# Long convolution with gate: how the last six results of the first phase reach the first two loads of the middle phase

## The chip, the cores and the metric

The kernel runs on one core of one Trainium2 chip. Five engines work side by side, each through its own list in order: TensorE (PE, with its weight loads PEld), VectorE (DVE), ScalarE (ACT), GpSimd (POOL) and SyncE (SP). SP, ACT and POOL issue DMAs, each on a queue of its own (in the profile q1 is SP's, q10 ACT's, q0 POOL's); all three queues are served by the same 16 DMA engines. The metric is the device time of one execution in microseconds (us).

## The reference, cut to what matters

```
h_filt = relu(pos_emb @ w1) @ w2 * exp(-0.01 * pos)      # a filter as long as the sequence
u      = x * v                                           # batch 4, sequence 12800, 128 channels
y      = irfft(rfft(u, 2S) * rfft(h_filt, 2S))[:S]       # long convolution, by FFT
x1     = x * y
gate   = sigmoid(causal conv of x1, 5 taps);  out = (gate * (x1 @ w_val)) @ w_out
```

The kernel computes the FFTs as matrix products in two steps: the sequence is cut into 2 halves (J) x 100 (N1) x 64 (N2).

## The kernel before

The program has three phases, each with an order written out by hand.

**First phase** (`signal()` and `filt()`, interleaved step by step). `signal()` runs over n = 0..63 (called n2). For each n, `prep(n)` makes the products and their sums and differences on DVE, PE transforms over N1 (L392, `fp`), ACT copies the two PSUM tiles into a result tile `st` of 128 partitions x 2 x 1024 (L393), and the tile goes to the DRAM tensor `a_u`. `a_u` is indexed [k, row, 1024] with k = 0..99; n fills the two rows `n%2*64 + n//2*2` and the next, so even n fill rows 0 to 63 and odd n rows 64 to 127. The 100 values of k stand scattered over the 128 partitions of `st` (PARTS: 64 of them in every second partition, 32 in every fourth, 4 in every 32nd), so a store is three DMAs: 64 k's by ACT and 32 by POOL (L401), and 4 by POOL an n later (L416, `flush`). For the last two n the store of ACT is cut: k = 0..3 go by SP, the other 60 by ACT. Two result tiles are not of the rotating `st` buffers: n = 61 writes into a spare input buffer (`xv_104` below) and n = 63 into the load buffer `ld_78`.

**Middle phase.** It runs over p = 0..49, pairs of k (2p and 2p+1). `load_a(p, parts)` (L198) loads k = 2p, 2p+1 of `a_u` into one of six buffers `ld`, 4 KB for each row and k; `spectrum` multiplies on PE (L492, `z_ps`): its first half uses partitions 0 to 63 (the even n), its second half partitions 64 to 127 (the odd n). DVE multiplies the result with the filter's spectrum (`times`, L498: `va`, `vb`, `vc`, `vd`), POOL adds (L579, L582), PE transforms back (L508, L531), POOL combines (L543), and the results go to the DRAM tensors `c_y` and `c_z`. One p takes DVE about 6.7 us.

**The border.** Pairs 0 and 1 are loaded in four DMAs each: EARLY is rows 0 to 55 and 64 to 119 (all n up to 55), LATE the rest. Pair 0's EARLY loads stand in SP's list at n = 58. LATE of pair 0 and all of pair 1 stand behind the first phase (p = -1), then pairs 2 and 3 whole. Also at p = -1, PE has the filter of pair 0 (`filter_pair`, L473) and ten products that only keep it busy (L565, `w_ps`) in front of `spectrum(0, 0)`. SP runs its list in order: a DMA that waits holds all behind it.

**Last phase**: it reads `c_y` and `c_z`, transforms over N1, and does gate, value and output products. The change doesn't touch it.

Of the kernel before, what the change touches and what calls it, by code (L numbers as in the profile page):

```python
# [24 lines left out]
J, N1, N2 = 2, 100, 64  # L25
# [6 lines left out]
PARTS = ((0, 64, 2, 0), (64, 32, 4, 1), (96, 4, 32, 3))  # L32
# [86 lines left out]
def tile_longconv_gate(  # L119
# [20 lines left out]
    nc = tc.nc  # L140
# [27 lines left out]
    def buffer(until):  # L168
        i = min(free_at, key=free_at.get)
        free_at[i] = until  # L170
        return LD[i]
# [14 lines left out]
    BD = B * D  # L186
    NP = N1 // 2
    PG = KG // 2
    EARLY, LATE = (slice(0, 56), slice(64, 120)), (slice(56, 64), slice(120, 128))
    weights, loaded = {}, {}  # L190

    def load_w(p):
        n_p = min(PG, NP - p)
        wt = buffer(p + n_p + 0.9)[:, 0:PG * 3 * 128].rearrange("p (k c e) -> p k c e", k=PG, c=3)
        nc.sync.dma_start(out=wt[:, 0:n_p], in_=t_w[:, p:p + n_p])
        weights[p // PG] = wt

    def load_a(p, parts, eng=nc.sync):  # L198
        if p not in loaded:
            loaded[p] = buffer(p - 0.2).rearrange("p (k j e) -> p k j e", k=2, j=J)  # L200
        a2 = loaded[p]
        eng.dma_start(
            out=a2[parts].rearrange("p k j e -> p k (j e)"),
            in_=a_u[2 * p:2 * p + 2, parts].rearrange("k p e -> p k e"))
# [5 lines left out]
    with tc.tile_pool(name="p1", bufs=1) as p1, tc.tile_pool(name="ps1", bufs=1, space=PSUM) as ps1:  # L210
# [10 lines left out]
        def load_pos(c0):  # L221
            if c0 < N2:
                for j in range(J):
                    sync_s.dma_start(out=pos_at(c0)[:, j], in_=pos_v[j][:, c0:c0 + HC])
# [83 lines left out]
        def fetch(upto=N2):  # L308
            while ring and fetched[0] < upto:
                i, t = ring.pop(0)  # L310
                n = fetched[0]
                for k0, k, step, p0 in PARTS:
                    nc.sync.dma_start(out=t[p0:p0 + step * (k - 1) + 1:step], in_=xv[n, k0:k0 + k])
                ahead.append((i, t))
                if i < 4:
                    free_at[i] = n - 2 * N2
                fetched[0] += 1
# [40 lines left out]
        def signal():  # L358
            fetch(4)
            load_pos(0)  # L360
            fetch()
            load_pos(HC)
            ready = [prep(0)]
            for n in range(N2):
                if n == 8:
                    nc.gpsimd.dma_start(out=dft, in_=t_dft)
                    nc.gpsimd.dma_start(out=tw, in_=t_tw)
                    nc.gpsimd.dma_start(out=inv, in_=t_inv)
                if n == 12:
                    for dst, src in ((wval, w_val), (wout, w_out), (cw, conv_w.rearrange("k d -> d k"))):  # L370
                        raw = p1.tile(list(dst.shape), mybir.dt.int64, name=f"raw{len(raws)}")
                        nc.gpsimd.dma_start(out=raw, in_=src)
                        raws.append((dst, raw))
                if n in (18, 22, 26):
                    _narrow(nc, p1, *raws[n // 4 - 4])
                if n == BACK + 2:
                    load_w(0)
                if n == N2 - 6:
                    for part in EARLY:
                        load_a(0, part)  # L380
                if n + 1 < N2:
                    ready.append(prep(n + 1))
                both = ready.pop(0)
                if n in SPARE:
                    st = next(t for i, t in ring if i == SPARE[n]).rearrange("p (c e) -> p c e", c=2)
                else:
                    st = p1.tile([128, 2, J * BD], F32, name="st", bufs=4)
                for c in range(2):
                    fp = ps1.tile([128, J, BD], F32, name="fp", bufs=2)
                    for j in range(J):  # L390
                        h = slice(j * 64, j * 64 + 64)
                        nc.tensor.matmul(out=fp[:, j], lhsT=fsd[h, c], rhs=both[c][h], start=True, stop=True)  # L392
                    nc.scalar.copy(out=st[:, c], in_=fp.rearrange("k j e -> k (j e)"))  # L393
                    yield
                src = st.rearrange("k c e -> k (c e)")
                row = n % 2 * N2 + n // 2 * 2
                dst = a_u[:, row:row + 2].rearrange("k c e -> k (c e)")
                for eng, (k0, k, step, p0) in zip((nc.scalar, nc.gpsimd), PARTS):
                    cuts = [0, 4, k] if k0 == 0 and n >= N2 - 2 else [0, k]
                    for a, b in zip(cuts, cuts[1:]):  # L400
                        (nc.sync if b == 4 else eng).dma_start(  # L401
                            out=dst[k0 + a:k0 + b], in_=src[p0 + step * a:p0 + step * (b - 1) + 1:step])
                if n % 2 == 1:
                    release()
                rest.append((dst, src))
                if len(rest) > 1 or n + 1 == N2:
                    flush()

        rest, raws = [], []
        SPARE = {N2 - 3: 6, N2 - 1: 3}  # L410

        def flush():
# [50 lines left out]
    with tc.tile_pool(name="p2", bufs=1, reuse_waits="tile") as p2, \  # L463
# [20 lines left out]
        def new_z():  # L484
            return ps2.tile([128, 2, BD], F32, name="z_ps", bufs=2)
# [67 lines left out]
        with tc.manual_schedule():  # L553
            for p in range(-1, NP + 2):
                now, nxt, old = 0 <= p < NP, p + 1 < NP, 0 <= p - 1 < NP
                if p < 0:
                    z_first = new_z()
                    for part in LATE:
                        load_a(0, part)
                    for part in EARLY + LATE:  # L560
                        load_a(1, part)
                    filt_p[0] = filter_pair(0)
                    for _ in range(10):
                        w_ps = ps2.tile([128, 2, BD], F32, name="c_ps", bufs=2)
                        nc.tensor.matmul(  # L565
                            out=w_ps[:, 0, 0:2 * D], lhsT=ident, rhs=dft.rearrange("p a k -> p (a k)"), start=True, stop=True)
                if (p + 3) % PG == 0 and p + 3 < NP:
                    load_w(p + 3)
                for q in range(2, AHEAD) if p < 0 else (p + AHEAD,):
                    if q < NP:  # L570
                        load_a(q, slice(0, 2 * N2))
                if now:
                    h = filt_p.pop(p)
                    z0, z1 = z_p.pop((p, 0)), z_p.pop((p, 1))
                    va = p2.tile([128, 2 * J, B, D], F32, name="va", bufs=3)
                    vb = p2.tile([128, 2 * J, B, D], F32, name="vb", bufs=2)
                    times(va, z0[:, 0], h[:, 0], 2 * J)
                    times(vb, z0[:, 1], h[:, 1], 2 * J)
                    (nc.gpsimd if nxt else nc.vector).tensor_tensor(va[:, 0:2], va[:, 0:2], vb[:, 0:2], op=ALU.add)  # L579
                    apart = p % 6 == 5  # L580
                    if not apart:
                        nc.gpsimd.tensor_tensor(va[:, 2:4], va[:, 2:4], vb[:, 2:4], op=ALU.add)  # L582
                if nxt:
                    z_p[p + 1, 0] = spectrum(p + 1, 0, z_first if p < 0 else None)
                if now:
                    vc = p2.tile([128, 2, B, D], F32, name="vc", bufs=2)
                    vd = p2.tile([128, 2, B, D], F32, name="vd", bufs=2)
                    times(vc, z1[:, 0], h[:, 0, 0:2], 2)
                    times(vd, z1[:, 1], h[:, 1, 0:2], 2)
                    v_p[p] = [va[:, 2:4]] + [vb[:, 2:4]] * apart + [vc, vd]  # L590
                if now and not nxt:
                    inverse(p, va[:, 0:2])
                if old:
                    inverse_half(p - 1, v_p.pop(p - 1))
                if p + 2 < NP:
                    filt_p[p + 2] = filter_pair(p + 2)
                if nxt:
                    z_p[p + 1, 1] = spectrum(p + 1, 1)
                if now and nxt:
                    inverse(p, va[:, 0:2])  # L600
                if 0 <= p - 2:
                    butterfly(p - 2)
                for s, c, i in early.get(p, ()):
                    load_part(s, c, i)
# [9 lines left out]
    with tc.tile_pool(name="p3", bufs=1, reuse_waits="tile") as p3, \  # L614
# [154 lines left out]
        with tc.manual_schedule():  # L769
# [10 lines left out]
            for i in range(-LEAD, (NT - 1) * R):  # L780
                t, r = divmod(i, R)
                s, q = divmod(i + LEAD, R)
                if q == 0 and s < NT:
                    if 3 <= s + 1 < NT:
                        load_rows(s + 1, (0, 1, 2))
                    j, g = y_order[s]
# [22 lines left out]
                if t + 1 >= 0:  # L809
                    j, g = groups[t + 1]  # L810
# [9 lines left out]
            t = NT - 1  # L820
# [63 lines left out]
```

## Time and profile before

| what | us |
|---|---|
| device time, median of 3 runs (1063.89 to 1065.49) | 1064.03 |
| the profiled execution's own device time | 1066.52 |
| its span, first to last instruction | 1064.7 |
| PE busy, share of the span | 978.8 (92%) |
| DVE busy | 966.9 (91%) |
| POOL busy | 747.9 (70%) |
| ACT busy | 649.2 (61%) |
| first product of the middle phase on DVE starts at | 323.58 |
| last product of the middle phase on DVE starts at | 671.96 |

All times below are us from the start of the span, of this one execution. A row of the timeline gives start, duration, engine, line, operation, what is written and read, and how often; in brackets the idle time of the engine before it and what ended it. An engine name with a q (SPq, ACTq) is that engine's sequencer, which issues DMAs. A row of the chain of waits gives start, duration and what the time was spent on. A row of the table by stretches gives, behind the stretch, its length, then the busy time of PE, PEld, DVE, ACT and POOL, then the granted clock of TensorE, the mean busy share of the 16 DMA engines, and GB/s.

### The profile page before, as it was taken

What the parts mean: (1) busy time and instruction counts of PE and PEld (TensorE: products, weight loads), DVE (VectorE), ACT (ScalarE), POOL (GpSimd) and SP (SyncE); (2) the same over time, 40 slices, a digit from 0 to 9 for tenths busy, and PEclk for the clock granted to TensorE, in tenths of its full rate; (3) what the DMA queues carried; (4) which work ended last, traced back from release to release, by engine and by line L of the source; (5) the groups of instructions that cost most, each with busy time, mean ns of one, the idle gap of its engine ahead of it and who ended that gap; (6) DMA issues with size and microseconds to landing.
All of it is one profiled execution on the core that took longest, in us unless ns stands there. A gap on an engine that the chain in (4) does not pass through costs nothing.

```text
span 1064.7 us, 21554 instructions
## 1 busy us (share of the span) xinstructions
PE 978.8 (92%) x8100; PEld 515.6 (48%) x8100; DVE 966.9 (91%) x933; ACT 649.2 (61%) x1145; POOL 747.9 (70%) x465
## 2 busy tenths in 40 slices
PE   2778799999988999999999999689999999999996
PEld 0344466566644545555445545334444444444442
DVE  8878999699948999999989999369999999999997
ACT  1445577788852444444444434277887888878784
POOL 2232222222225999999899999679999999999990
PEclk9989899999997999999999999899999999999999
DMA  8999899988989889989999997977888888888813
GB/s 286 383 352 375 330 381 373 397 315 327 393 273 306 318 302 334 341 314 339 333 311 342 345 334 259 333 285 270 312 286 300 284 295 306 282 299 296 299 72 124
DMA packets 97152, 330.16 MB, mean 310 GB/s; under 512 B 12691, under 2 KB 37883, under 8 KB 81051
## 3 DMA queue, kind: packets, MB, share of 16 engines
q1 hardware_dynamic: 41864, 196.96, 54.1%
q10 hardware_dynamic: 49506, 111.30, 27.0%
q0 software_dynamic: 5680, 20.53, 5.1%
q8 instruction: 66, 1.08, 0.4%
q14 instruction: 36, 0.29, 0.1%
HBM read 197.67 MB, written 131.07 MB: 309 GB/s over the span
## 4 chain that ended last, share of the span: by engine, by line
PE 65%; DMA 13%; DVE 7%; POOL 5%; ACT 4%; issue 4%; SPq 1%; ACTq 1%; DVEq 0%; POOLq 0%
PE sd L672 11%; PE o_ps L738 8%; PE v_ps L728 7%; PE c_ps L531 7%; PE fp L392 6%; PE tp L684 6%; PE c_ps L508 6%; PE z_ps L492 5%; DMA xv<-in_xv_dram 4%; DMA ld<-in_xv_dram 3%; PE gp L293 3%; PE ap L267 3%; DMA c_z<-c_both 2%; DVE vb L498 2%; POOL c_both L543 2%
## 5 line engine op out<-in xcount | busy, mean ns | idle before, releaser
L699 POOL TENSOR_TENSOR ext<-yr,xr 128x400 f32<-128x400 f32 x120 | 308.3, 2570 | 23.2 <-DVE yr L697 10.8
L716 DVE SCALAR_TENSOR_TENSOR gt<-ext,cw,gt 128x1600 f32<-128x1600 f32 (+1 forms) x132 | 242.3, 1835 | 0.1
L401 POOL DMA_DIRECT2D a_u<-st x62 | 33.3, 537 | 222.9 <-ACT st L393 219.1
L393 ACT COPY st<-fp 128x1024 f32<-128x1024 f32 x124 | 125.7, 1029 | 81.6 <-PE fp L392 41.4
L672 PE MATMUL sd<-ld,inv 128*64 128x512 f32 x512 | 128.0, 619 | 7.2 <-DMA ld<-c_y 6.7
L543 POOL TENSOR_TENSOR c_both<-c_raw 128x512 f32<-128x512 f32 x100 | 126.6, 1295 | 9.9 <-DMA c_z<-c_both 6.4
L536 ACT COPY c_raw<-c_ps 128x1024 f32<-128x1024 f32 x50 | 50.8, 1015 | 135.3 <-PE c_ps L531 117.9
L498 DVE TENSOR_TENSOR va<-z_ps,h_sb 128x2048 f32<-128x2048 f32 x50 | 114.1, 2282 | 19.7 <-PE z_ps L492 19.6
L579 POOL TENSOR_TENSOR va<-va,vb 128x1024 f32<-128x1024 f32 x49 | 117.0, 2387 | 20.4 <-DVE vb L498 20.4
L498 DVE TENSOR_TENSOR vb<-z_ps,h_sb 128x2048 f32<-128x2048 f32 x50 | 114.2, 2284 | 12.8 <-POOL va L582 12.8
L492 PE MATMUL z_ps<-ld,ld 64*64 64x512 f32 x800 | 111.6, 614 | 10.2 <-DVE vb L498 6.1
L392 PE MATMUL fp<-ld,fsd 64*128 64x512 f32 x320 | 89.4, 663 | 27.3 <-DVE ld L343 14.5
L738 PE MATMUL o_ps<-gd,wout 128*128 128x400 f32 x256 | 107.8, 503 | 6.1 <-DVE gd L733 4.6
L677 ACT COPY sd_sb<-sd 128x512 f32<-128x512 f32 x128 | 76.9, 601 | 49.4 <-PE sd L672 37.8
L728 PE MATMUL v_ps<-ext,wval 128*128 128x400 f32 x252 | 105.4, 501 | 0.0
L508 PE MATMUL c_ps<-va,ld 64*64 64x512 f32 x800 | 98.1, 604 | 4.0 <-POOL va L579 2.5
L582 POOL TENSOR_TENSOR va<-va,vb 128x1024 f32<-128x1024 f32 x42 | 101.0, 2406 | 0.0
L684 PEld LDWEIGHTS tp<-ident,sd_sb 128*128 128x128 f32 x512 | 58.3, 140 | 77.8 <-PE sd L672 45.4
L697 DVE TENSOR_TENSOR yr<-tp,dif 128x400 f32<-128x400 f32 x128 | 72.5, 566 | 25.8 <-ACT dif L687 21.6
L514 ACT COPY c_sb<-c_ps 128x1024 f32<-128x1024 f32 x49 | 49.7, 1014 | 59.5 <-PE c_ps L508 59.5
L684 PE MATMUL tp<-ident,sd_sb 128*128 128x128 f32 x512 | 80.0, 280 | 4.0 <-DVE yr L697 4.0
L733 DVE TENSOR_TENSOR gd<-v_ps,sg 128x400 f32<-128x400 f32 x126 | 71.4, 567 | 0.2 <-ACT sg L721 0.2
(116 smaller groups left out, 1817.7 us busy)
## 6 DMA issues: line engine op xcount, KB each, us to landing
ld<-a_u SPq DMA_DIRECT2D x48, 1024.0 KB
a_u<-st ACTq DMA_DIRECT2D x61, 512.0 KB
xr<-in_xt_dram SPq DMA_DIRECT2D x32, 800.0 KB
c_y<-c_sb ACTq DMA_DIRECT2D x49, 512.0 KB
out_dram<-o_sb ACTq DMA_DIRECT2D x31, 800.0 KB
c_z<-c_both ACTq DMA_DIRECT2D x48, 512.0 KB
ld<-in_xv_dram SPq DMA_DIRECT2D x40, 512.0 KB
ld<-c_y SPq DMA_DIRECT2D x32, 512.0 KB
```

What stands on the lines that cost most here:

```text
L392: nc.tensor.matmul(out=fp[:, j], lhsT=fsd[h, c], rhs=both[c][h], start=True, stop=True)
L393: nc.scalar.copy(out=st[:, c], in_=fp.rearrange("k j e -> k (j e)"))
L492: nc.tensor.matmul(out=z[half[h], c], lhsT=wk[half[c], 0, half[h]], rhs=a2[half[c], h, j], start=True, stop=True)
L498: nc.vector.tensor_tensor(out, z.rearrange("p (b d) -> p b d", d=D).unsqueeze(1).to_broadcast([128, n, B, D]), h_sb.unsqueeze(2).to_broadc ...
L508: nc.tensor.matmul(out=c_ps[half[m], h], lhsT=wk[half[h], 1 + c, half[m]], rhs=vt[half[h], c].rearrange("p b d -> p (b d)"), start=(c == 0 ...
L543: nc.gpsimd.tensor_tensor(both[:, :, m], raw[:, :, 1], raw[:, :, 0], op=op)
L672: nc.tensor.matmul(out=to, lhsT=inv[:, 2 if j * m * c else c], rhs=t, start=True, stop=True)
L684: nc.tensor.transpose(out=tp[:, b], in_=t[:, b], identity=ident)
L699: nc.gpsimd.tensor_tensor(e[:, r0 + r], yr, xr, op=ALU.mult)
L716: nc.vector.scalar_tensor_tensor(gt, rows(t, k)[:, cols], cw[:, k:k + 1], gt, op0=ALU.mult, op1=ALU.add)
L728: nc.tensor.matmul(out=v_ps, lhsT=wval, rhs=rows(t)[:, r * ROW:(r + 1) * ROW], start=True, stop=True)
L738: nc.tensor.matmul(out=o_ps, lhsT=wout, rhs=gd, start=True, stop=True)
```

## The change

EARLY becomes rows 0 to 57 and 64 to 121 (all n up to 57), and LATE is gone. For n = 58 to 63, the four k's of pairs 0 and 1 no longer go through `a_u`: SP copies them from the result tile straight into the two load buffers, four DMAs for each n (k = 0..3), each of one partition of the tile into two partitions (2 x 4 KB). Pair 0's EARLY loads stand in SP's list at n = 60 (before: n = 58), then the copies of n = 58, 59 and 60, then pair 1's EARLY loads (before: behind the first phase), then the copies of n = 61, 62 and 63. The stores of n = 58 to 63 to `a_u` leave out k = 0..3; from n = 60 on ACT issues none of them and POOL all; those of n = 62 stand behind the tile of n = 63.

```diff
-    EARLY, LATE = (slice(0, 56), slice(64, 120)), (slice(56, 64), slice(120, 128))
+    EARLY = slice(0, 58), slice(64, 122)
...
+    def new_a(p):
+        loaded[p] = buffer(p - 0.2).rearrange("p (k j e) -> p k j e", k=2, j=J)
...
-                if n == N2 - 6:
+                if n in (N2 - 4, N2 - 3):
                     for part in EARLY:
-                        load_a(0, part)
+                        load_a(n - N2 + 4, part)
...
-                for eng, (k0, k, step, p0) in zip((nc.scalar, nc.gpsimd), PARTS):
-                    cuts = [0, 4, k] if k0 == 0 and n >= N2 - 2 else [0, k]
-                    for a, b in zip(cuts, cuts[1:]):
-                        (nc.sync if b == 4 else eng).dma_start(
-                            out=dst[k0 + a:k0 + b], in_=src[p0 + step * a:p0 + step * (b - 1) + 1:step])
+                if n >= N2 - 6:
+                    direct.append((row, st))
+                while direct and n >= N2 - 4:
+                    at, t = direct.pop(0)
+                    for k in range(4):
+                        if k // 2 not in loaded:
+                            new_a(k // 2)
+                        nc.sync.dma_start(
+                            out=loaded[k // 2][at:at + 2, k % 2].rearrange("c j e -> c (j e)"), in_=t[2 * k:2 * k + 1])
+                held.append((dst, src))
+                while held and not n == N2 - 2:
+                    d, u = held.pop(0)
+                    for eng, (k0, k, step, p0) in zip((nc.scalar if n < N2 - 4 else nc.gpsimd, nc.gpsimd), PARTS):
+                        a = 4 if k0 == 0 and n >= N2 - 6 else 0
+                        eng.dma_start(out=d[k0 + a:k0 + k], in_=u[p0 + step * a:p0 + step * (k - 1) + 1:step])
...
-                    for part in LATE:
-                        load_a(0, part)
-                    for part in EARLY + LATE:
-                        load_a(1, part)
```

SP's list at the border before, from pair 0's EARLY loads on. `ld_80` is pair 0's buffer, `ld_77` pair 1's, `ld_78` first the tile of n = 63 and then pair 2's buffer. DMAHW0 to DMAHW7 are the eight counters on which the DMAs of SP and ACT report their landing, taken in turn; a DMA waits until the one that used its counter before has landed:

```order
L202 DMA ld_80<-a_u 56x2x1024 [waits DMAHW6_49,DMAHW3_49]
L202 DMA ld_80<-a_u 56x2x1024 [waits DMAHW4_49,DMAHW2_49]
L401 DMA a_u<-st 4x2048 [waits DMAHW2_49,Activation_49]
L202 DMA ld_80<-a_u 8x2x1024 [waits DMAHW6_49,DMAHW5_49,DMAHW7_49,DMAHW3_49,DMAHW2_49]
L401 DMA a_u<-ld_78 4x2048 [waits DVE_49,Activation_49]
L202 DMA ld_80<-a_u 8x2x1024 [waits DMAHW6_49,DMAHW5_49,DMAHW0_49]
L202 DMA ld_77<-a_u 56x2x1024 x2
L202 DMA ld_77<-a_u 8x2x1024 [waits DMAHW1_49]
```

The same place of SP's list now (L205 is `load_a`, L408 the new copies): pair 0's two loads and the copies of n = 58 and 59:

```order
L205 DMA ld_80<-a_u 58x2x1024 [waits DMAHW6_49,DMAHW3_49]
L205 DMA ld_80<-a_u 58x2x1024 [waits DMAHW4_49,DMAHW2_49]
L408 DMA ld_80<-st 2x1x1024 [waits Activation_49]
L408 DMA ld_80<-st 2x1x1024 [waits DMAHW7_49]
L408 DMA ld_77<-st 2x1x1024 [waits DMAHW0_49]
L408 DMA ld_77<-st 2x1x1024 [waits DMAHW1_49]
L408 DMA ld_80<-st 2x1x1024 [waits DMAHW3_49,Activation_49]
L408 DMA ld_80<-st 2x1x1024 [waits DMAHW4_49]
```

The last two rows take the counters DMAHW3 and DMAHW4 of the two loads at the top, and so wait for these to land. The copies of n = 60 follow; then come pair 1's loads and the copies of n = 61 (`xv_104`), 62 (`st`) and, of n = 63 (`ld_78`), those for pair 0:

```order
L205 DMA ld_77<-a_u 58x2x1024 [waits DMAHW3_49]
L205 DMA ld_77<-a_u 58x2x1024 [waits DMAHW4_49]
L408 DMA ld_80<-xv_104 2x1x1024 [waits DMAHW5_49,DVE_49,Activation_49]
L408 DMA ld_80<-xv_104 2x1x1024 [waits DMAHW6_49]
L408 DMA ld_77<-xv_104 2x1x1024 [waits DMAHW7_49]
L408 DMA ld_77<-xv_104 2x1x1024 [waits DMAHW0_49]
L408 DMA ld_80<-st 2x1x1024 [waits DMAHW1_49,Activation_49]
L408 DMA ld_80<-st 2x1x1024 [waits DMAHW2_49]
L408 DMA ld_77<-st 2x1x1024 [waits DMAHW3_49]
L408 DMA ld_77<-st 2x1x1024 [waits DMAHW4_49]
L408 DMA ld_80<-ld_78 2x1x1024 [waits DMAHW5_49,DVE_49,Activation_49]
L408 DMA ld_80<-ld_78 2x1x1024 [waits DMAHW6_49]
```

Here too the copies of n = 62 for pair 1 wait on DMAHW3 and DMAHW4, which are pair 1's two loads now, and the copies of n = 63 for pair 0 stand behind them. Eight DMAs of rows that lay behind the first phase have become 4 loads and 24 copies inside it; on PE and DVE the order of instructions is the same as before.

More of the change, by code (lines that the diff above doesn't have):

```diff
@@ L196, in load_w @@
         weights[p // PG] = wt
+    def new_a(p):
+        loaded[p] = buffer(p - 0.2).rearrange("p (k j e) -> p k j e", k=2, j=J)
     def load_a(p, parts, eng=nc.sync):
         if p not in loaded:
-            loaded[p] = buffer(p - 0.2).rearrange("p (k j e) -> p k j e", k=2, j=J)
+            new_a(p)
         a2 = loaded[p]
@@ L407, in signal @@
                     flush()
-        rest, raws = [], []
+        rest, raws, held, direct = [], [], [], []
         SPARE = {N2 - 3: 6, N2 - 1: 3}
```

## The prediction

> **What bounds the kernel now.** I read the chain of waits first, at the border of first and middle phase, since the change moves nothing else. Columns: start, duration, what.
>
> ```profile
> 310.50 1.03 ACT ld L393
> 311.53 0.02 issue
> 311.55 5.47 DMA a_u<-ld
> 317.01 0.02 SPq L202
> ...
> 317.06 4.30 DMA ld<-a_u
> 321.36 0.14 issue
> 321.50 0.48 PE z_ps L492
> ```
>
> The last result tile (n = 63) is ready at 311.53. Then SP's store of its k = 0..3 takes 5.47 us to land, pair 0's last load of 8 rows takes 4.30 us, and only then PE does the second half of the first spectrum, at 321.50. The timeline of DVE and PE says who waits:
>
> ```profile
> 313.67 2.86 PE L565 MATMUL c_ps<-dft,ident 128*128 128x256 f32 x12 [0.52 <-ACT h_sb L481]
> 316.46 1.07 PE L492 MATMUL z_ps<-ld,ld 64*64 64x512 f32 x4
> 323.58 2.29 DVE L498 TENSOR_TENSOR va<-z_ps,h_sb 128x2048 f32<-128x2048 f32 x1 [18.87 <-PE z_ps L492]
> ```
>
> DVE stands still for 18.87 us until 323.58. What it starts then is the bound of the next 350 us, as the groups of DVE over the middle phase show:
>
> ```profile
> L498 DVE TENSOR_TENSOR vb<-z_ps,h_sb 128x2048 f32<-128x2048 f32 x50 | 114.2, 2284 | 12.8 <-POOL va L582 12.8
> L498 DVE TENSOR_TENSOR va<-z_ps,h_sb 128x2048 f32<-128x2048 f32 x50 | 114.1, 2282 | 19.7 <-PE z_ps L492 19.6
> ```
>
> Of the 19.7 us of `va`, 18.87 are the border; beyond it DVE idles some 13.7 us in 350, and waits for POOL then, which hangs on DVE in turn. So **a shift of 323.58 shifts the end by as much**, and the question is only when pair 0's last rows (those of n = 63) are in its buffer.
>
> **What the change removes.** The round trip through DRAM, 5.47 + 4.30 us, is replaced by one copy inside the core. If that were all, the limit would be PE's busy-keeping products, which end at 316.46 here and some 2 us earlier where ACT issues no stores, and the end would come up to 9 us sooner. But the copies of n = 63 stand last in SP's list, and four loads have come in front of them.
>
> **What the loads cost.** How a DMA spreads over the 16 engines can be counted: each engine that takes part adds one small packet to mark its end. Of the first 4 us of the program and of a stretch of the middle phase, the DMA view gives (queue: packets, MB, share of 16 engines):
>
> ```profile
> q10 hardware_dynamic: 364, 0.30, 23.4%
> ...
> fsd<-in_tab_sd_dram ACTq DMA_DIRECT2D x1, 128.0 KB
> fwd<-in_tab_fwd_dram ACTq DMA_DIRECT2D x1, 117.2 KB
> win<-in_tab_win_dram ACTq DMA_DIRECT2D x1, 50.0 KB
> ```
>
> ```profile
> DMA packets 720, 3.01 MB, mean 402 GB/s; under 512 B 48, under 2 KB 48, under 8 KB 720
> ...
> q1 hardware_dynamic: 720, 3.01, 101.5%
> ```
>
> In the second, three loads of 128 rows make 48 marks, 16 each. In the first, `fsd` has 128 rows and `fwd` and `win` 100 each, 328 packets of data; the other 36 are marks: 16 + 10 + 10. So 100 rows went over 10 engines, not 16: rows are dealt in equal whole shares. 56 rows then go over 14 engines (14 x 4), and the table by stretches, while pair 1's two loads of 56 rows were alone in front (DMA share and GB/s are last), agrees:
>
> ```profile
> 320.00:321.00 1.00, 0.00 (x0) 0.00 (x0) 0.00 (x0) 0.00 (x0) 0.00 (x0) 0.67 0.87 197
> 322.00:323.00 1.00, 1.00 (x10) 0.49 (x6) 0.00 (x0) 0.00 (x0) 0.00 (x0) 0.50 0.88 188
> ```
>
> 14/16 is 0.875; and since both loads were queued, the second didn't use the two engines that the first left idle: DMAs of one width take the same engines. **58 is 2 x 29; the only equal shares up to 16 are 2.** So each of the four new loads would run on two engines, the same two, and so would the 24 copies of two rows, queued behind them.
>
> The Trainium skill, page "DMA: Bandwidth & Descriptors", section "Why a DMA increments its semaphore by 16 and not by 1", says the same in general: a DMA uses the largest number of engines up to 16 that divides its slowest dimension, on SP's and ACT's queues the lowest-numbered ones. By that rule 58 rows get 2 engines, always the same; this trace agrees with it for 128, 100 and 56 rows, and shows no DMA of 58.
>
> The price: a load of 58 rows x 2 x 4 KB is 475 KB, 238 KB on each of two engines. The stretch above moved 402 GB/s at a share of 101.5%, so 24.8 GB/s by engine: **9.6 us a load**, 38.4 for four. A fast end is 26.5 GB/s, from the first phase:
>
> ```profile
> 265.00:270.00 5.00, 5.00 (x35) 3.42 (x32) 4.97 (x8) 4.57 (x9) 1.11 (x2) 1.00 1.01 424
> ```
>
> That makes 9.0 us a load, 2.5 less in all. The slow end takes 14 engines at 197 GB/s, 14.1 each, as above: 16.9 us a load, 29 more in all. I take 9.6, of whole loads of the same 4 KB rows; in the slow row 14 engines write one half of the partitions at once, two would not press as hard.
>
> **The sum.** The two new loads of pair 0 need the stores of n = 56 and 57. When that of n = 57 lands is told by SP's own wait for that counter in the present kernel; the other rows are SP's issues, and landings of stores:
>
> ```profile
> 291.44 2.17 SPq L202 DMA_DIRECT2D ld<-a_u  x2
> L401 SPq EVENT_SEMAPHORE  x2: 17/17/17, 298.1 to 311.1; - x2
> L202 SPq DMA_DIRECT2D ld<-a_u x12: 271/355/494, 291.4 to 332.9; - x12
> DMA to landing us min/median/max: 3.0/5.9/8.1
> ```
>
> - The second load of pair 0 starts at 298.1 (now 293.3), about when the last inputs of the first phase leave the engines, so I let the two engines start on the loads there.
> - SP's list decides the order. The copies of n = 59 wait on the counters of pair 0's loads, so SP stands until these have landed. After them 8 issues of about 0.4 us (0.355 and a wait) come before both loads of pair 1 are out: 3.2 us in which the two engines have no load. Then the copies of n = 62 for pair 1 wait on the counters of pair 1's loads, and behind them stand the copies of n = 63.
> - So four loads run one after the other: 38.4 us.
> - The same engines also carry their sixteenth of the stores of n = 58 to 63: 96 rows of 8 KB each, 49 KB by engine, 2.0 us at 24.8 GB/s, 11.9 for six. Part may fall into the 3.2 us; I count half of the gap, 1.6.
> - 298.1 + 38.4 + 11.9 + 1.6 = 350.0: pair 1's second load has landed. Three issues to the second copy of n = 63: 1.2. Its landing: 3.0, the shortest landing of the row above; the end of range is the 5.47 of the chain. PE starts the second half at 354.2, and DVE follows 323.58 - 321.50 = 2.08 later: **356.3, 32.7 us later than now**.
>
> Every other edit hides under that. ACT loses four issues, so n = 63 is done some 2 us earlier, and waits for nothing of SP's. POOL issues four more DMAs of about 0.53 us and is free until DVE's first `vb`; if the wait at SP went, these issues would still be done near 313. The loads of pairs 2 and 3 stand behind n = 63's copies, at about 352, and take 2.6 us each at 402 GB/s; pair 2 is needed some 11 us behind DVE's start:
>
> ```profile
> 334.96 1.09 PE L492 MATMUL z_ps<-ld,ld 64*64 64x512 f32 x8
> ```
>
> TensorE's clock is at half (0.50 above) when the second half starts today, so a longer idle adds no cold start that isn't in the 2.08 already.
>
> Against its own execution (1066.52 us of device time, 1.8 of it around the span) the sum is 1099.2. That execution lies 2.5 above the median of the runs, 1064.0; carried to that, the forecast is **1096.7 us**.
>
> **The rivals.**
> - *Wide loads, faster.* If the 58 rows spread as 56 do, a load takes 2.4 us at 197 GB/s. Pair 0's second load lands near 304 (298.1 + 2.4 + 3.0), the eight issues end near 307, pair 1's second load lands near 315 (4.8, 3.0 of landing), the copy of n = 63 near 319, DVE starts at 321.2: 2.4 us sooner, 1061.6. Were nothing of it late, PE's busy products would be the limit and it would be 1055. It decides if the two engines' counting is wrong; the 36 marks speak against it. 14%, a part of it within 0.2%.
> - *Narrow, but on different engines.* If each narrow DMA took another pair of engines, the two loads of a pair would run side by side: pair 0's land near 312 with some stores between, pair 1's go out at 315 and land near 328, n = 63 near 332, DVE 334.3: 10.7 later, 1075. Against it: the share of 0.87 to 0.88 with two loads queued. 8%.
> - *Narrow and slow.* Two engines at 14.1 GB/s each: 1126. Or the two engines serve the stores in longer turns. 12% for all beyond 1102.
>
> **How the numbers follow.** The forecast has 66%; its own range is 1088 (early start of the first load by 4 us, 9.0 a load, no gap) to 1102 (full gap, landing 5.47). With the narrow loads on different engines, and half of the slow ones, 80% lie between 1073 and 1108. 0.2% is about what a measurement of this kernel can tell from no change. Slower by more: 66 + 8 + 12 = 86%; faster 11% and the same 3%, out of the first rival.
>
> **What would show it.** Right: SP standing in two long waits (some 20 us each) at the third and fourth copy group, DMA share near 0.13 between about 330 and 350, DVE's first product waiting some 50 us, first `z_ps` halves far apart, and all behind shifted as a block. Wrong: a DMA share over 0.8 while only these loads run, SP through with its copies by 320, or a DVE start before 323.58. If the start moves but the end doesn't, the claim that the middle phase only shifts is wrong.

## The result, and the profile after

The changed kernel takes **1104.04 us** (median of 3 runs, 1102.63 to 1106.36) against 1064.03: 1.0373 times as long, 95% interval 1.0346 to 1.0400. The profiled execution takes 1106.36 us, its span is 1104.6. The forecast was 1096.7, with 1088 to 1102 as the range of its own mechanism and 1073 to 1108 as the wider one.

The timeline of DVE at the border, now (start, duration, engine and line, what, and the idle time before it):

```profile
305.84 2.50 DVE L346 TENSOR_TENSOR ld<-ld 128x512 f32<-128x512 f32 x4
364.09 2.29 DVE L511 TENSOR_TENSOR va<-z_ps,h_sb 128x2048 f32<-128x2048 f32 x1 [55.75 <-PE z_ps L505]
```

and before, DVE's last work of the first phase:

```profile
302.21 2.50 DVE L343 TENSOR_TENSOR ld<-ld 128x512 f32<-128x512 f32 x4
```

DVE stands **55.75 us where it stood 18.87: 36.9 more**. Its last work of the first phase ends 3.63 us later than in the profile of before. That isn't the change: a cast of the weights far ahead of it already starts 4.5 us later, in a part of the program that is the same in both.

```profile
109.40 0.23 DVE L96 CAST rest<-tmp 128x128 f32<-128x128 int32 x1
```

```profile
113.91 0.23 DVE L96 CAST rest<-tmp 128x128 f32<-128x128 int32 x1
```

The first row is of before, the second of after; over the thirteen profiles of this case that cast starts between 108.71 (e7, which has most of the change) and 113.91. So the idle time at the border, not a start on the clock, is the measure of what follows. The two executions differ by 39.84 us: 36.9 of idle, 3.6 from the first phase, and the rest (-0.7) behind. DVE's groups over the middle phase (busy and mean, then idle time before) show that nothing else moved there:

```profile
L511 DVE TENSOR_TENSOR vb<-z_ps,h_sb 128x2048 f32<-128x2048 f32 x50 | 114.2, 2284 | 13.7 <-POOL va L591 13.7
L511 DVE TENSOR_TENSOR va<-z_ps,h_sb 128x2048 f32<-128x2048 f32 x50 | 114.1, 2282 | 55.8 <-PE z_ps L505 55.8
```

Where the 55.75 us go stands in the chain of waits (start, duration, what):

```profile
301.40 32.35 DMA ld<-a_u
...
333.76 0.56 SPq L408
...
338.03 0.42 SPq L205
...
338.50 0.54 SPq L205
...
339.15 6.03 SPq L408
...
347.25 12.62 DMA ld<-st
...
359.92 2.61 PE z_ps L505 x6
```

Pair 0's second load (L205) takes from 301.40 to 333.75. Seven copies (L408) at 0.60 us follow (an eighth, the first of n = 59, waited for the first load alone and went out at 316.9), then pair 1's loads at 338.03. A copy of n = 62, issued at 347.25, lands at 359.87, when pair 1's second load has landed too; only then PE starts. SP's own timeline, in two pieces, shows that last landing from the other side:

```profile
347.25 3.07 SPq L408 DMA_DIRECT2D ld<-st  x3
```

```profile
358.82 0.56 SPq L408 DMA_DIRECT2D ld<-st  x1
359.49 2.36 SPq L408 DMA_DIRECT2D ld<-ld  x4
```

The fourth copy of n = 62 is issued at 358.82, when the counter of pair 1's second load is free, and the four of n = 63 (`ld<-ld`) behind it. SP's waits, from 285 us to 372 (us in total, times, longest), put it in one row:

```profile
SPq L408 <- DMA ld<-a_u: 28.7, 4, 16.3
```

These are the waits for a semaphore alone. Two issues took long besides: the 6.03 us at 339.15 above, and the first copy behind pair 0's loads, as the copies from 301 to 330 us show (in ns, least, median and most):

```profile
L408 SPq DMA_DIRECT2D ld<-st x5: 558/558/9385, 301.7 to 316.9; - x5
```

The table by stretches (DMA share and GB/s are last), while these loads run alone, pair 0's second in the first row and pair 1's in the others:

```profile
326.00:331.00 5.00, 0.00 (x0) 0.00 (x0) 0.00 (x0) 0.00 (x0) 0.00 (x0) 0.50 0.13 44
339.00:346.00 7.00, 0.00 (x0) 0.00 (x0) 0.00 (x0) 0.00 (x0) 0.00 (x0) 0.50 0.12 44
350.00:358.00 8.00, 0.00 (x0) 0.00 (x0) 0.00 (x0) 0.00 (x0) 0.00 (x0) 0.50 0.13 52
```

0.13 of 16 is two engines, at 22 to 26 GB/s each.

### The profile page after: what moved, and what is told of

It reads as the page before. It is cut to its first block, busy times and chain, and to the rows that moved or that the text cites. A ratio compares the mean times of both kernels' runs of the same rounds, so it can differ in the third digit from the quotient of the medians.

```text
span 1104.6 us, 21579 instructions
## 1 busy us (share of the span) xinstructions
PE 977.1 (88%) x8100; PEld 515.6 (47%) x8100; DVE 966.7 (88%) x933; ACT 649.1 (59%) x1145; POOL 749.8 (68%) x469
## 4 chain that ended last, share of the span: by engine, by line
PE 55%; DMA 21%; DVE 7%; POOL 6%; ACT 4%; issue 4%; SPq 2%; ACTq 1%; DVEq 0%; POOLq 0%
PE sd L681 11%; PE o_ps L747 7%; PE v_ps L737 7%; PE tp L693 6%; PE c_ps L544 5%; DMA c_z<-c_both 5%; DMA a_u<-st 4%; PE c_ps L521 4%; PE z_ps L505 4%; PE fp L395 4%; DMA ld<-in_xv_dram 4%; DMA ld<-a_u 3%; POOL va L591 2%; POOL c_both L556 2%; DMA xv<-in_xv_dram 2%
## 5 line engine op out<-in xcount | busy, mean ns | idle before, releaser
L511 DVE TENSOR_TENSOR vb<-z_ps,h_sb 128x2048 f32<-128x2048 f32 x50 | 114.2, 2284 | 13.7 <-POOL va L591 13.7
L706 DVE TENSOR_TENSOR yr<-tp,dif 128x400 f32<-128x400 f32 x128 | 72.8, 569 | 24.8 <-ACT dif L696 20.9
```

The costliest lines, as they stand in the source:

```text
L511: nc.vector.tensor_tensor(out, z.rearrange("p (b d) -> p b d", d=D).unsqueeze(1).to_broadcast([128, n, B, D]), h_sb.unsqueeze(2).to_broadc ...
```

## The experiments

Theory A is that of the prediction: 58 rows run on two engines, always the same, which everything else at the border shares. Theory B: SP's list (waits on counters, 24 copies in one queue) is the loss, however wide the loads. The ratios are to the kernel before, timed beside each run; the idle times are of one profiled execution each.

| run | ratio, 95% interval | DVE idle at the border, us |
|---|---|---|
| changed kernel | 1.0373, 1.0346 to 1.0400 | 55.75 |
| e1, loads as 56 + 2 | 1.0039, 1.0016 to 1.0063 | 22.29 |
| e2, loads as 29 + 29 | 1.0661, 1.0612 to 1.0709 | 88.07 |
| e3, before with 58 rows | 1.0305, 1.0266 to 1.0345 | 29.21 + 21.33 |
| e4, pair 1's loads last | 1.0385, 1.0335 to 1.0434 | 39.05 + 22.29 |
| e5, pair 0's copies only | 0.9984, 0.9964 to 1.0003 | 12.03, and 4.12 ahead of it |
| e6, 56 + 2, pair 1 last | 1.0023, 1.0000 to 1.0047 | 19.68 + 1.05 |
| e7, 56 + 2, stores on ACT | 1.0039, 1.0022 to 1.0056 | 23.33 |
| e8, e5 with pair 1's loads behind | 1.0013, 0.9994 to 1.0032 | 20.32 |
| e9, no late stores | timed once, 1103.59 us | 39.36 |
| e10, e5 with pair 1's loads early | 0.9997, 0.9977 to 1.0018 | 16.31 |
| e11, before with pair 1's loads early | 1.0002, 0.9981 to 1.0022 | 18.57 |

### The width of the loads: e1 and e2

```diff
 # e1
-    EARLY = slice(0, 58), slice(64, 122)
+    EARLY = slice(0, 56), slice(56, 58), slice(64, 120), slice(120, 122)
 # e2
-    EARLY = slice(0, 58), slice(64, 122)
+    EARLY = slice(0, 29), slice(29, 58), slice(64, 93), slice(93, 122)
```

> Each 58-row load of the changed kernel is split into one of 56 rows and one of 2; everything else stays. Theory A (58 rows run on two engines, and that alone is the loss): a 56-row load takes 14 engines, some 2.4 to 3.5 us instead of 9 to 19, pair 1's rows have landed near 316, SP is through with its copies near 319, DVE stands some 16 to 18 us at the border instead of 55.75, and the time is about 1062 (1056 to 1067). Theory B (the loss is SP's list: waits on counters and 24 copies in one queue, however wide the loads are): the time stays above 1090, DVE idle above 40 us.

> Each 58-row load is split into two of 29 rows, a prime number; same bytes, same places in SP's list, four issues more. Theory A: 29 rows run on one engine each, and always the same one, so the loads of a pair take 4 x 237 KB on one engine, some 36 to 40 us instead of 20; 32 to 42 us are added and the time is 1136 to 1150. Theory A2 (narrow, but each load on other engines): two loads of 29 side by side are as good as one of 58, the time stays within 1098 to 1110. Theory B (only the order of SP's list counts): 1104 to 1108 for four issues more.

The same bytes in other widths: e1 takes 33.5 of the 36.9 us back, and e2 adds 32.3 to the 55.75. The chain of e2 has pair 1's loads:

```profile
350.80 6.20 SPq L205
...
357.05 31.36 DMA ld<-a_u
```

The first of them is issued at 349.79 (the end of the copies), the last lands at 388.40: 38.6 us for 950 KB, 24.6 GB/s. The DMA view of e2 from 362 to 369, while they run (queue: packets, MB, share of 16 engines):

```profile
q1 hardware_dynamic: 45, 0.18, 6.4%
```

6.4% of 16 is one engine. Theory A holds, and A2 falls: four loads of 29 rows in a row all use that one. The time, 1135.85 us, is at the lower edge of A's 1136 to 1150. Theory B falls with both.

What A did not foresee in e1 is the remainder, 22.29 us where 16 to 18 were expected (the time, 1069.74, is above its 1056 to 1067). Its chain:

```profile
309.38 7.76 DMA ld<-a_u
...
317.16 0.78 SPq L408
...
318.04 5.95 DMA ld<-ld
...
324.04 0.65 PE z_ps L505
```

SP still waits for a load of pair 1 (2 rows, 7.76 us with the others ahead of it) before the last copy of n = 62, and the first copy of n = 63 then takes 5.95 us to land. The wide loads shrink the wait that the prediction named; it doesn't go.

### The loads of 58 rows without the copies: e3

```diff
-    EARLY, LATE = (slice(0, 56), slice(64, 120)), (slice(56, 64), slice(120, 128))
+    EARLY, LATE = (slice(0, 58), slice(64, 122)), (slice(58, 64), slice(122, 128))
```

> The kernel before, with its early loads of 58 rows instead of 56 and its late ones of 6 instead of 8: no direct copies, no moved stores, pair 1's loads behind the first phase as before. Theory A: pair 0's loads run on two engines from 291 and 298 on and land near 320 to 332 between the stores, pair 1's near 350, where before it was 326; the second pair of DVE's products is late by some 20 us, and the time is about 1088 (1078 to 1095). Theory B (the direct copies and SP's waits on them are the loss): 1062 to 1068, as before.

Two rows more in the early loads of the kernel before (and two fewer in the late ones), with nothing else of the change, cost 3.05%. DVE stands at the border and again before the second pair:

```profile
333.85 2.29 DVE L498 TENSOR_TENSOR va<-z_ps,h_sb 128x2048 f32<-128x2048 f32 x1 [29.21 <-PE z_ps L492]
361.93 2.29 DVE L498 TENSOR_TENSOR va<-z_ps,h_sb 128x2048 f32<-128x2048 f32 x1 [21.33 <-PE z_ps L492]
```

At the border, the chain has SP's store of n = 62's four k's, which stands behind pair 0's loads and takes 17.01 us to land; in the kernel before, SP's next load, which waits for that store, goes out 2.3 us after it (308.50 to 310.80).

```profile
308.81 17.01 DMA a_u<-st
```

That is A's mechanism, though the time lies above its range (1097.88 against 1078 to 1095). The likely reason for the excess is the one worked out for e4 below.

### Pair 1's loads last in SP's list: e4

```diff
-                if n in (N2 - 4, N2 - 3):
+                if n == N2 - 4:
                     for part in EARLY:
-                        load_a(n - N2 + 4, part)
+                        load_a(0, part)
...
+                if n + 1 == N2:
+                    for part in EARLY:
+                        load_a(1, part)
                 held.append((dst, src))
```

> The changed kernel with pair 1's two loads behind the copies of n = 63 in SP's list, so that pair 0's last copies wait for pair 0's loads only. Theory A (the two engines' bytes are the limit): pair 0 starts some 18 us sooner (DVE idle about 37 us), but pair 1's loads still need some 20 us on two engines and DVE stands a second time; the time is 1090 to 1098. Theory B (the order of SP's list is the loss, not the engines): 1080 to 1085, the whole 20 us of the second pair's loads gone.

Both theories missed: pair 0 starts 16.7 us sooner, as A had it (39.05 against 55.75), but the time, 1107.37 us, isn't lower. The chain has the reason:

```profile
342.82 28.54 DMA ld<-a_u
...
371.40 0.48 PE z_ps L508
```

Pair 1's second load lands 29.0 us after the first was issued (342.35 to 371.36); in the changed kernel it was 20.8. Three loads of 128 rows, for pairs 2 to 4, now stand right behind it, each with 65.5 KB on every engine: 2.6 us at 24.8 GB/s, 7.9 for three. 20.8 + 7.9 = 28.7. (A fourth load, of 768 KB, goes out at 357.24 and isn't in this sum.) That the later loads of the same queue share the engines with the earlier one is worked out from these numbers, and no run tests it by itself; in e3, with the same three loads behind, the first load of 6 rows, which stands behind pair 1's two of 58, has 28.30 in the chain:

```profile
331.14 28.30 DMA ld<-a_u
```

So the order of SP's list only chooses who waits; the two engines' bytes are the limit.

### The stores on the same engines: e9

```diff
-                while held and not n == N2 - 2:
+                while held and n < N2 - 6:
                     d, u = held.pop(0)
...
+                if 20 <= n < 26:
+                    row = n % 2 * N2 + (n + 38) // 2 * 2
+                    d = a_u[:, row:row + 2].rearrange("k c e -> k (c e)")
+                    for k0, k, step, p0 in PARTS:
+                        nc.gpsimd.dma_start(out=d[k0:k0 + k], in_=src[p0:p0 + step * (k - 1) + 1:step])
...
-                rest.append((dst, src))
+                if n < N2 - 6:
+                    rest.append((dst, src))
```

> The changed kernel without the stores of n = 58 to 63: these rows of the scratch tensor are filled from the tiles of n = 20 to 25 instead, early in the first phase, so that pairs 2 to 49 compute with other data and the same work. It asks how much of the 36 us of pair 0's two loads is the stores on the same two engines. Theory A (stores and loads share the two engines): the two loads together take 19 to 22 us instead of 36, as pair 1's do, and DVE stands some 14 us less, about 42. Theory D (the loads of pair 0 are slow by themselves): they still take over 30 us and DVE stands over 50.

The chain of e9:

```profile
315.63 16.36 DMA ld<-a_u
```

```profile
310.50 5.37 SPq L205 DMA_DIRECT2D ld<-a_u  x2
```

The second row is SP's timeline: pair 0's loads are issued from 310.50 on and have landed at 331.99, 21.5 us. In the changed kernel they take from 297.4 to 333.75, 36.4. Theory A: the stores of n = 58 to 63 are 14.9 us of it, and DVE stands 16.4 us less (39.36). The end doesn't show this (1103.59 us, timed once), because DVE's wait begins at 321.5 (360.90 - 39.36) instead of 308.3. The added stores of n = 20 to 25 lie in that longer first phase and are the likely cause; no run separates them.

### What the straight copies are worth: e6, e7, e5, e8, e10, e11

With 56 + 2 rows, e6 takes e4's order of pair 1's loads, and e7 gives the stores back to ACT:

```diff
 # e7, on e1
-                    for eng, (k0, k, step, p0) in zip((nc.scalar if n < N2 - 4 else nc.gpsimd, nc.gpsimd), PARTS):
+                    for eng, (k0, k, step, p0) in zip((nc.scalar, nc.gpsimd), PARTS):
```

> The changed kernel with both repairs: loads split into 56 + 2 rows, and pair 1's loads behind the copies of n = 63. All 24 copies and the stores on POOL stay. Theory A (the 22.29 us of idle time that are left with the split alone come from SP waiting on the counters of pair 1's loads ahead of n = 63's copies): n = 63's copies are issued at once, DVE stands 14 to 16 us, the time is 0.2 to 0.5 per cent under the kernel before. Theory C (the 24 narrow copies themselves): DVE stands over 20 us and the time is 0.2 to 0.5 per cent over the kernel before, as with the split alone.

> The split of 56 + 2 rows, with the large stores of n = 60 to 63 issued by ACT again instead of POOL. If the move of the stores costs nothing, as the prediction has it, the time stays within 2 us of the split alone (ratio 1.002 to 1.006). Rival: POOL's queue of stores slows the loads and copies at the border, and the ratio falls to 1.000 or below.

e7 is as expected: the stores' move costs nothing that is seen. e6 falls between its theories with 19.68 us of idle time, and its ratio of 1.0023 is C's. The wait on pair 1's loads is gone, but the copies of n = 61 and 62, with only stores beside them, take longer to issue:

```profile
309.19 0.56 SPq L408
...
309.80 1.68 SPq L408
...
312.18 2.20 SPq L408
...
314.42 1.38 SPq L408
...
315.85 2.14 SPq L408
```

That is up to 2.20 us of SP for a copy, 0.56 when the engines are quiet.

The next three start from the kernel before and copy only pair 0's rows of n = 60 to 63; a load of 4 + 4 rows brings n = 56 to 59. They differ in the place of pair 1's loads of 56 rows: where the scheduler put them in e5, ahead of the last input rows; behind n = 63's copies in e8; behind pair 0's in e10.

```diff
+    MID = slice(56, 60), slice(120, 124)
...
+                if n == N2 - 2:
+                    for part in MID:
+                        load_a(0, part)
...
+                if n >= N2 - 4:
+                    direct.append((row, st))
+                while direct and n >= N2 - 2:
+                    at, t = direct.pop(0)
+                    for k in range(2):
+                        nc.sync.dma_start(
+                            out=loaded[0][at:at + 2, k].rearrange("c j e -> c (j e)"), in_=t[2 * k:2 * k + 1])
...
 # e8
+                if n + 1 == N2:
+                    for part in EARLY:
+                        load_a(1, part)
 # e10 and e11 (e11 without the copies and MID)
                 if n == N2 - 6:
-                    for part in EARLY:
-                        load_a(0, part)
+                    for q in range(2):
+                        for part in EARLY:
+                            load_a(q, part)
```

> The kernel before, with its loads of 56 rows, its stores and its place for pair 1 as they were; only pair 0's rows of the last four n2 (60 to 63) are copied straight, in 8 copies with nothing of pair 1 ahead of them, and a load of 4 + 4 rows brings those of n = 56 to 59. Theory A (a direct copy saves the round trip if no load of pair 1 stands ahead of it in SP's list): the copies of n = 63 are issued when the tile is ready, land 2 to 3 us later, the second half of the first spectrum starts when PE's busy products end, DVE stands 14 to 15.5 us instead of 18.87, and the time is 0.3 to 0.5 per cent under the kernel before. Theory C (copies of two rows cost as much as the round trip, by their two engines): no difference, within 0.2 per cent.

> As the kernel that copies only pair 0's rows of n = 60 to 63 straight, but with pair 1's two loads of 56 rows written behind the copies of n = 63; there they had come ahead of the first phase's last input rows, and DVE had stood 4.12 us for those. Theory A: the 4.12 us are gone, DVE stands 14 to 16 us at the border (18.87 before), and the time is 0.3 to 0.5 per cent under the kernel before. Theory C (copies of two rows are worth no more than the round trip once all is in order): within 0.2 per cent.

> Pair 0's rows of n = 60 to 63 straight (8 copies), pair 1's loads of 56 rows directly behind pair 0's, before the last tiles: nothing but stores is left beside the copies at the border. Theory A (the copies were slow, 6.7 and 10.4 us, because pair 1's loads and the stores shared their two engines): n = 63's copies land 4 to 6 us after issue, DVE stands 14.5 to 17 us, the time is 0.2 to 0.4 per cent under the kernel before. Theory C (two engines under the stores alone make a copy as slow as the round trip): DVE stands 18 us or more, within 0.2 per cent.

> Control: the kernel before with pair 1's two loads of 56 rows directly behind pair 0's, and no copy at all. If a gain of the run beside it comes from the straight copies, this one stays within 0.2 per cent of the kernel before (DVE 17.5 to 20 us); if it comes from the loads' new place, it gains as much.

e5 stands least at the border, but 4.12 us more ahead of it, for input rows that came behind pair 1's loads; its gain is 0.16 per cent, where A had 0.3 to 0.5, and isn't clear of zero. e8 takes the 4.12 us away, and the copy of n = 63 becomes as slow as the round trip that it replaces (5.47 + 4.30 us), as C has it (ratio 1.0013):

```profile
309.85 0.58 SPq L407
...
310.48 10.44 DMA ld<-ld
```

In e10 the copies are off the chain:

```profile
292.31 13.95 DMA ld<-a_u
...
306.28 0.02 ACTq L413
...
314.43 3.29 PE c_ps L575 x14
317.72 1.11 PE z_ps L504 x7
```

Here a store that ACT issues waits for the counter of pair 1's early load (292.31 + 13.95), and PE comes to the first spectrum when its own busy-keeping products end. DVE stands 16.31 us, 2.3 less than in e11, the control. That is 0.2% of the time, and neither ratio differs from 1 by more than its interval: the gain is seen in the idle time, not shown in the time. Set against each other, the twelve runs of e10 are 1.8 us below the twelve of e11 on average, with a 95% interval from 3.8 below to 0.1 above: near the 2.3 us, but not clear of zero. A's idle time of 14.5 to 17 us holds for e10, its gain of 0.2 to 0.4 per cent over the kernel before isn't measured. No version tried beats the kernel before by more than can be measured; e5 comes nearest.

## Why the prediction was right, step by step

- **58 rows on two engines, always the same: right.** Share 0.12 to 0.13 with one or two such loads in the queue; e2 halves the engines and doubles the loads; e1 undoes nearly all of the loss; e3 makes most of it (3.05 of 3.73%) with this one edit. Of the rivals, *narrow, but on different engines* falls with e2. *Narrow and slow* falls in its first form: 22 to 26 GB/s for each engine when alone, where 24.8 was taken and 14.1 feared. Its second form, longer turns for the stores, isn't ruled out: 14.9 us by e9 where 11.9 were counted. The Trainium skill, page "DMA: Bandwidth & Descriptors", section "Why a DMA increments its semaphore by 16 and not by 1", has the rule of the divisor; the shares of 0.13 for 58 rows and 6.4% for 29 agree with it.
- **Four loads one after the other, by SP's list: right in the sum, not in its form.** Two long waits of some 20 us at the third and fourth group of copies were foretold. SP stood instead in four waits, the longest 16.3 us, and 9.39 and 6.03 us while issuing a copy, and the halves of the first spectrum came close together, not far apart: the copies of n = 62, too, stood behind pair 1's loads. And e4 shows that the order was not what cost: with pair 1's loads behind, the bytes on the two engines wait for each other all the same.
- **The sum, term by term.** From the start of pair 0's second load to the landing of pair 1's, 51.9 us were counted and 57.4 measured (301.40 to 358.8):

| term | counted | measured |
|---|---|---|
| pair 0's loads and the stores, from the second load's start | 19.2 + 11.9 = 31.1 | 32.35 |
| gap between the loads | 1.6 | 4.3 (333.75 to 338.03) |
| pair 1's loads | 19.2 | 20.8 |
| landing to DVE's start | 6.3 | 5.3 |

- **The mis-sized term is the gap.** Eight issues were priced at 0.4 us, and half of that was put under the stores. Seven lay in the gap, a copy's issue takes 0.60 us with what lies around it, and the stores were over before it (share 0.13 from 326 on), so that none of it was hidden. That is 2.7 of the 4.2 us by which the idle time was under-forecast (32.7 + 18.87 = 51.6 against 55.75). Pair 1's loads give 1.6 more, pair 0's with the stores 1.25; the last term takes 1.0 back. The stores, too, were small in the sum: 11.9 counted, 14.9 by e9, part of it before the second load's start. The prediction dealt them evenly over 16 engines. By its own rule of equal shares, 60 rows go over 15 engines and 4 rows over 4, and two engines could carry 57 KB of a tile instead of 49; that estimate gives 13.9 us for six, and no run tests it.
- **The range: right only in its wider form.** 1104.04 us lies 2 us above the 1088 to 1102 that the prediction gave to its own mechanism (whose upper end comes to 1100.8 by its own terms, 1096.7 + 1.6 + 2.5), and within the 1108 that it had added for half of the slow rival. So the mechanism is borne out by the experiments, while that the time fell within the range owes something to the margin for another.
- **A shift of DVE's start shifts the end: right**: no other idle time of DVE's middle phase grew by more than 1 us (`vb` 12.8 before, 13.7 after). The medians differ by 40.0 us. With 36.9 at the border, the rest is within what one first phase differs from another (3.6 us in the two profiles); the forecast had nothing for it.
- **Every other edit hides: right** for the stores on POOL, as far as e7 shows it with the loads split; the others weren't tested one by one.
- **The rival of wide loads was sized wrong.** It had 1061.6 us, 2.4 us under the kernel before; e1, the nearest case that was measured, lies 0.39% above it. The step at fault is "the copy of n = 63 near 319": a copy was priced at 3.0 us to land, the shortest of a row of stores, and in e1 it takes 5.95; and pair 1's last load, on which SP waits ahead of it, lands there at 317.14 (309.38 + 7.76) and not near 315. The other limit there, PE's busy-keeping products, is real: e10 reaches it.

## What to carry to other kernels

Choose the number of rows of a DMA by its divisors before its bytes: 58 rows for 56 took a load from 14 engines to 2, and two rows more cost 3%. Price a direct copy that saves a trip through DRAM by the traffic of its moment on its own few engines (5.95 us in e1, 10.44 in e8), not by what it takes in a quiet queue. Where several DMAs share a counter or an engine, moving one in the list moves the wait to another; look for who issues behind it.

## What the runs showed of the hardware that was not expected

- **Issuing a DMA can take ten times its usual time and more.** Behind two narrow loads, SP's issue of one copy took 9.39 us in the changed kernel and of another 6.03 (339.15 in its chain), that of the third load of pair 1 took 6.20 in e2 (350.80), and behind stores a copy's took up to 2.20 in e6, against 0.56 when quiet. The profile has these as issuing, not as waiting for a semaphore. That the engines' queues were full is a guess; no run separates it from other causes.
- **Loads behind a narrow one seem to lengthen it.** Pair 1's two narrow loads took 29.0 us to land with three wide ones behind them in the same queue (e4), and 20.8 with none (the changed kernel), though the wide ones were issued later.
- **A copy of 8 KB can take 10.44 us to land** (e8), when stores were issued before it and two loads of 56 rows behind it.
